# Reordering the start, thinning one bias sum and splitting the last eviction of a tuned Fourier-mixing and expert kernel

## The chip, the cores and the metric

One core of one Trainium2 chip. The metric is device time in microseconds (us), median over executions; a profiled execution gives a trace, whose span is about 1.8 us shorter than the time of the same execution, as it leaves out the launch. All runs told of here were of state fast, or single runs, with a mean granted clock of TensorE of 0.994 or more. Even so, the runs of the kernel before lie in two clusters on every chip used, at 853.0 to 853.9 and 854.5 to 855.9, so a difference of 0.1% needs several runs and an interval.

## The reference, cut to what matters

```python
# x: (8, 3008, 256) float32; out: (24064, 256) float32
X = np.fft.rfft(x, axis=1)                  # along the 3008 positions
Yr = Xr @ w_r - Xi @ w_i + b_r              # 256 x 256, complex
Yi = Xr @ w_i + Xi @ w_r + b_i
Y  = soft_threshold(Yr, 0.01) + 1j * soft_threshold(Yi, 0.01)
x  = np.fft.irfft(Y, n=3008, axis=1).reshape(24064, 256)
h  = x @ w_in                               # 256 x 2048
g  = s * np.maximum(h, 0)**2 + b            # s, b scalars
out = g @ w_out                             # 2048 x 256
```

As b is a scalar, `b @ w_out` is b times the column sums of w_out: one row, added to every row of the result. Those sums are the "bias" of this text.

Names that come up again: x is loaded by batch, so "the third x" is the input of the third batch. F_c and T_c are the tables of the forward and the inverse transform, and the first F matmul (L432, L433 in the changed kernel) is the first that uses F_c and the result of the mixing by W. ring, vd and vs are buffers of later transform stages. `us`, set in this type, is a tile of the kernel and not the microsecond; in the quoted texts, "us" with no figure ahead of it means this tile. A cold array is one for which the trace shows a granted clock of 0.5.

## The kernel before

The transform of 3008 is split into 94 x 32. Batch 0 goes through it by itself, in the head (0 to 52 us). From then on TensorE works through tiles of 512 tokens (first matmul by w_in, Relu on ScalarE, square on VectorE, second matmul by w_out), and the transforms of the next batches are slipped in between as units, at slots of a plan. One slot is one of the 16 slices of the first matmul.

The first stage of batch 0, with W (w_r and w_i) loaded only after the first chunk has been copied:

```python
    def first_batch():
        ut = ypool.tile([P, DC, 96, N2], F16, name="ut", tag="yt")
        keep_awake(36)                           # idle matmuls that warm the array
        for c in range(N2 // XCH):               # 4 chunks of x
            for dc in range(DC):
                ps = two_banks()
                for j in range(XCH):
                    ... matmul(ps[:, j // 4, ...], x16[(0, c)][...], A_t ...)
                for h in range(2):               # two copies out of one two-bank tile
                    evac(ut[:, dc, :, n2 : n2 + 4], ps[:, h, 0:384]...)
            keep_awake(14 if c < 3 else 10)
            if c == 0:
                ... memset(st[0:1, :, 0:D:P], 0.0)   # holds W until VectorE is here
                emit_load_w()
            if c == 1: ... emit_load_forward()       # F_c
            if c == 2: ... emit_load_inverse()       # T_c
            if c == 2: place_w(0)
        place_w(1)
        ...
```

The bias, the second matmul's end and the plan (cuts marked with dots):

```python
    def make_bias():
        ps = other_bank()
        for q in range(MC):                      # 16 matmuls of 256 columns
            nc.tensor.matmul(ps[:, 0:D], ones, w_out_t[:, q, :],
                             start=(q == 0), stop=(q == MC - 1))
        ...
        def mm(sub, mc):                         # a sub-tile is 128 tokens
            h = sub % 2                          # two sub-tiles share a bank
            ...
            if mc == MC - 1 and (h == 1 or sub == nsub - 1):
                ... one VectorE instruction takes both out, then one store each
    ...
    plan.setdefault(15, []).append(make_bias)
    plan.setdefault(17, []).append(lambda: emit_load_x(2))   # third batch
    schedule(22, 44, s23_units(1))                           # second batch
```

The first stage of the second batch (s1_units) writes its result u to DRAM in four stores (ud) and reads it back in another layout in four loads (`us`); this way out and back is called the bounce of u. s23_units(1) starts with matmuls on `us`:

```python
            if j == XCH - 2:
                nc.sync.dma_start(out=ud[:, c * XCH : (c + 1) * XCH, :], in_=u[0:96])
            if i == N2 // 2 - 1:
                for q in range(4):
                    nc.sync.dma_start(out=t, in_=uv[:, 6 * q : 6 * q + 6, :])   # us
```

Of the kernel before, what the change touches and what calls it, by code (L numbers as in the profile page):

```python
# [9 lines left out]
F16 = mybir.dt.float16  # L10
F32 = mybir.dt.float32
# [3 lines left out]
P = 128  # L15
# [81 lines left out]
def kernel(  # L97
# [69 lines left out]
    def two_banks():  # L167
        return hpool.tile([P, 2, 512], F32, name="psh", tag="psh")
# [11 lines left out]
    def emit_load_x(b):  # L180
        xv = x[b].rearrange("(n1 n2) d -> n1 (n2 d)", n2=N2)
        for c in range(N2 // XCH):
            t = xpool.tile([P, XCH * D], F16, name="x16", tag="x16")
            nc.gpsimd.dma_start(  # L184
                out=t[0:N1, :], in_=xv[:, c * XCH * D : (c + 1) * XCH * D]
            )
            x16[(b, c)] = t

    ones = cpool.tile([P, P], F16, name="ones")
# [2 lines left out]
    def keep_awake(n):  # L192

        ps = other_bank()
        for _ in range(n):
            nc.tensor.matmul(ps[:, 0:P], ones, ones, start=True, stop=True)


    A_t = cpool.tile([P, 96], F16, name="A_t")
# [3 lines left out]
    w_st = []  # L203
    for w in (w_r, w_i):
        st = rpool.tile([P, DC, D], F32, name="w_st", tag="rt")
        w_st.append(st)

    def emit_load_w():

        for e in (slice(0, P), slice(P, D)):  # L210
            for w, st in zip((w_r, w_i), w_st):
                nc.sync.dma_start(
                    out=st[:, :, e], in_=w.rearrange("(c p) e -> p c e", p=P)[:, :, e]
                )


    b_g = cpool.tile([P, 2, D], F32, name="b_g")
    nc.vector.memset(b_g, 0.0)
# [52 lines left out]
    nc.vector.memset(T_t, 0.0)  # L271
    F_2 = [uspool.tile([P, H, P], F16, name="F_2", tag="us") for _ in range(2)]
    for f in F_2:
        nc.vector.memset(f, 0.0)

    def make_bounds():
        for t, c in ((low, -LAM), (high, LAM)):
            nc.gpsimd.tensor_scalar(
                out=t, in0=b_st, scalar1=-1.0, scalar2=c, op0=ALU.mult, op1=ALU.add
            )  # L280
# [8 lines left out]
    def blocks(t):  # L289
        return t.rearrange("p q (r a k) -> p q r a k", r=2, a=2)  # L290

    def place_w(ec):
        e = slice(ec * P, ec * P + P)
        for i in range(2):
            nc.scalar.copy(out=W_t[:, :, i, e], in_=w_st[i][:, :, e])

    def place_f(h):
        q = slice(h * H, h * H + H)
# [14 lines left out]
    def place_t(h):  # L313
        q = slice(h * H, h * H + H)
        for i in range(4):
            r = slice(32 * i, 32 * i + 32)
            c = 64 * (i % 2)
            nc.vector.tensor_copy(out=T_t[r, q, c : c + 64], in_=T_c[r, q])

    def make_bias():  # L320
        ps = other_bank()
        for q in range(MC):
            nc.tensor.matmul(
                ps[:, 0:D], ones, w_out_t[:, q, :], start=(q == 0), stop=(q == MC - 1)
            )
        for j in range(2):
            nc.scalar.activation(
                out=bias_bc[:, j], in_=ps[:, 0:D], func=AF.Copy, scale=bb_bc
            )
# [9 lines left out]
    def first_batch():  # L339
        ut = ypool.tile([P, DC, 96, N2], F16, name="ut", tag="yt")  # L340
        last_dve = last_act = None
        keep_awake(36)
        for c in range(N2 // XCH):
            for dc in range(DC):
                ps = two_banks()
                for j in range(XCH):
                    lo = j * D + dc * P
                    last_pe = nc.tensor.matmul(
                        ps[:, j // 4, (j % 4) * 96 : (j % 4) * 96 + 96],
                        x16[(0, c)][0:N1, lo : lo + P], A_t[0:N1, :],  # L350
                        start=True, stop=True,
                    )
                for h in range(2):
                    n2 = c * XCH + 4 * h
                    on_dve, on_act = evac(
                        ut[:, dc, :, n2 : n2 + 4],
                        ps[:, h, 0:384].rearrange("p (n k) -> p k n", k=96), 384,
                    )
                    last_dve = on_dve or last_dve
                    last_act = on_act or last_act  # L360
            with tc.issue_after(last_pe.ins):
                keep_awake(14 if c < 3 else 10)
            if c == 0:
                with tc.issue_after(last_dve.ins):
                    for st in w_st:
                        nc.vector.memset(st[0:1, :, 0:D:P], 0.0)
                emit_load_w()
            if c == 1:
                with tc.issue_after(last_dve.ins):
                    nc.vector.memset(F_c[0:1, 0, 0, 0:1], 0.0)  # L370
                emit_load_forward()
            if c == 2:
                with tc.issue_after(last_dve.ins):
                    nc.vector.memset(T_c[0:1, 0, 0:1], 0.0)
                emit_load_inverse()
            if c == 2:
                with tc.issue_after(last_act.ins):
                    place_w(0)
        with tc.issue_after(last_dve.ins), tc.issue_after(last_act.ins):
            place_w(1)  # L380
            place_f(0)
            place_f_2(0)

# [117 lines left out]
        for i in range(2 * U + 2):  # L501
            if i < 2 * U:
                mix(*steps[i])
            if 0 <= i - 1 < 2 * U:
                fwd_dft(*steps[i - 1])
            if 0 <= i - 2 < 2 * U:
                inv_dft(*steps[i - 2])
            k = i - U - 2
            if 0 <= k < 4:
                turn(0, k)  # L510
            if 0 <= k - 1 < 4:
                last_dft(0, 8 * (k - 1))
            if i >= 2 * U:
                some(3)
            if i == 0:
                with tc.issue_after(g_last[0].ins):
                    place_t(0)
            if i == 1:
                with tc.issue_after(g_last[0].ins):
                    place_f(1)  # L520
            if i == 2:
                with tc.issue_after(g_last[0].ins):
                    place_f_2(1)
            if i == 3:
                with tc.issue_after(g_last[0].ins):
                    place_t(1)
            if i == 9:

                gate = nc.gpsimd.tensor_copy(out=low[0:1, 0, 0:1], in_=vt[0:1, 1, 0, 0:1])
                with tc.issue_after(gate.ins):  # L530
                    make_w_g()
                    make_bounds()
        for k in range(4):
            turn(1, k)
            some(1)
            if k:
                last_dft(1, 8 * (k - 1))
# [269 lines left out]
    def second_mms(ti):  # L807
# [5 lines left out]
        hold = {}  # L813

        def mm(sub, mc):
            h = sub % 2
            if h == 0 and mc == 0:
                hold["ps"] = other_bank().rearrange("p (h e) -> p h e", h=2)
            ps = hold["ps"]
# [4 lines left out]
            )  # L824
            if sub == nsub - 1 and mc % 2 == 1:
                gts.pop((ti, mc // 2))
            if mc == MC - 1 and (h == 1 or sub == nsub - 1):
                k = h + 1
                ost = opool.tile([P, 2, D], F32, name="ost", tag="ost")
                nc.vector.scalar_tensor_tensor(  # L830
                    out=ost[0:size, 0:k], in0=ps[0:size, 0:k], scalar=s_bc[0:size],
                    in1=bias_bc[0:size, 0:k], op0=ALU.mult, op1=ALU.add,
                )
                load["dve"] += 0.12 + 0.27 * k
                for i in range(k):
                    store(tl, sub - k + 1 + i, ost[:, i, :])
# [73 lines left out]
```

## Time and profile before

| | before |
|---|---|
| time, three first runs | 853.37 us median (853.29 to 853.9) |
| span of the profile | 852.0 us |
| TensorE busy | 98% |
| mixing matmuls (L401) run freely from | 16.08 us |
| first unit of the second batch on TensorE | 67.42 us |
| last matmul ends, span ends | 846.76, 852.0 us |

In a profile line, L401 is a line of the kernel, PE is TensorE, PEld its weight loads, DVE VectorE, ACT ScalarE, POOL GpSimd, SPq the queue of DMA issues. "out<-in" are the program's names. A line of the chain reads: start, length, what the end of the program was waiting for at that time. A line of the timeline reads: start, length, engine, instruction, and in brackets the idle time before it and what ended it. The lines of the head, of the first expert tile and of the tail stand in the prediction.

### The profile page before, as it was taken

To read this page: it belongs to the slowest core of one execution; us is meant where nothing else is said; L and a number is where in the kernel's file an instruction comes from. 1 tells how busy PE (TensorE), PEld (TensorE's weight loads), DVE (VectorE), ACT (ScalarE), POOL (GpSimd) and SP (SyncE) were. 2 spreads that over 40 slices of the span, in tenths; PEclk is the share of its full clock that TensorE was granted. 3 is DMA by queue.
4 is the path that set the end of the run, shared out by engine and by line. 5 is a ranking of instruction groups with operands and counts; after the bars stand their busy time and mean duration, and the time that the engine had idled before them with its cause. 6 is when DMAs were issued, how large, how long until landed. Compare 5 with 4: busy or idle time off the path is not lost.

```text
span 852.0 us, 17108 instructions
## 1 busy us (share of the span) xinstructions
PE 836.7 (98%) x6668; PEld 602.7 (71%) x6668; DVE 698.1 (82%) x1027; ACT 643.8 (76%) x860; POOL 32.5 (4%) x54
## 2 busy tenths in 40 slices
PE   8899999999999999999999999999999999999997
PEld 7757777777777766777667776777667777766765
DVE  6888987888878987888878888888977888776674
ACT  5887887787778887787777887787877778666663
POOL 3210000000000000000000000000000000000000
PEclk9999999999999999999999999999999999999999
DMA  7963457424671357424663247613354223411111
GB/s 168 157 155 97 115 138 174 122 77 97 169 195 54 93 151 190 110 78 104 164 159 89 74 106 180 191 39 92 100 155 119 62 78 96 112 32 38 38 44 50
DMA packets 105410, 95.07 MB, mean 112 GB/s; under 512 B 9454, under 2 KB 97778, under 8 KB 103986
## 3 DMA queue, kind: packets, MB, share of 16 engines
q1 hardware_dynamic: 99330, 79.57, 32.3%
q0 software_dynamic: 6000, 14.42, 10.7%
q8 instruction: 52, 0.85, 0.4%
q14 instruction: 28, 0.23, 0.1%
HBM read 52.54 MB, written 46.66 MB: 116 GB/s over the span
## 4 chain that ended last, share of the span: by engine, by line
PE 90%; DVE 4%; ACT 3%; DMA 1%; issue 1%; DVEq 0%; ACTq 0%; POOLq 0%
PE psa L820 37%; PE psh L751 37%; PE psf L617 4%; PE psf L552 3%; PE psf L588 2%; PE psf L603 2%; PE psf L700 2%; PE psf L647 2%; DVE gt L765 1%; ACT rt L758 1%; PE psh L401 1%; DMA w_st<-in_w_r_dram 1%; DMA x<-in_x_dram 1%; ACT yt L160 0%; ACT vs L160 0%
## 5 line engine op out<-in xcount | busy, mean ns | idle before, releaser
L758 ACT ACTIVATE rt<-psh 128x1024 f32<-128x1024 f32 (+2 forms) x384 | 387.1, 1009 | 115.6 <-PE psh L751 114.2
L765 DVE TENSOR_TENSOR gt<-rt 128x1024 f16<-128x1024 f32 (+2 forms) x323 | 386.6, 1200 | 99.4 <-ACT rt L758 98.7
L820 PE MATMUL psa<-w_out_t,gt 128*128 128x256 f16 (+1 forms) x3024 | 453.9, 272 | 0.1
L820 PEld LDWEIGHTS <-gt 128*128 128x128 f16 (+1 forms) x3024 | 301.0, 101 | 186.8 <-issue 1.6
L751 PE MATMUL psh<-yt,w_in 128*128 128x512 f16 (+1 forms) x1344 | 396.9, 378 | 0.0
L751 PEld LDWEIGHTS <-w_in 128*128 128x128 f16 x1536 | 142.8, 98 | 26.6 <-issue 1.7
L830 DVE SCALAR_TENSOR_TENSOR ost<-psa,s_bc,bias_bc 128x512 f32<-128x512 f32 (+1 forms) x96 | 70.9, 738 | 9.6 <-PE psa L820 8.2
L762 ACT ACTIVATE gt<-rt 128x1024 f16<-128x1024 f32 (+2 forms) x61 | 64.1, 1051 | 1.0
L622 DVE TENSOR_TENSOR ring<-psf,s 128x512 f16<-128x512 f32 x84 | 57.5, 685 | 3.5 <-PE psf L617 3.4
L160 ACT CAST v<-psf 128x512 f16<-128x512 f32 x80 | 46.5, 582 | 18.1 <-PE psf L647 18.1
L160 ACT CAST xf<-psf 128x512 f16<-128x512 f32 x82 | 48.0, 585 | 11.1 <-PE psf L588 11.1
L160 ACT CAST u<-psf 96x512 f16<-96x512 f32 x78 | 45.1, 580 | 12.3 <-PE psf L552 12.1
L751 PE MATMUL psh<-tail,w_in 128*128 128x512 f16 (+1 forms) x192 | 52.1, 353 | 0.0
L617 PE MATMUL psf<-W_g,xf 128*128 128x256 f16 x336 | 50.4, 273 | 0.0
L160 ACT CAST yt<-psf 128x480 f16<-128x480 f32 (+2 forms) x76 | 38.5, 518 | 14.4 <-PE psf L700 14.3
L552 PE MATMUL psf<-x,A_t 94*96 94x512 f16 x104 | 39.6, 381 | 1.6 <-ACT yt L160 0.5
L628 DVE TENSOR_TENSOR ring<-ring,high 128x512 f16<-128x512 f16 x84 | 35.5, 423 | 2.2
L629 DVE TENSOR_TENSOR ring<-ring 128x512 f16<-128x512 f16 x84 | 35.5, 422 | 1.9
L627 DVE TENSOR_TENSOR ring<-ring,low 128x512 f16<-128x512 f16 x84 | 35.4, 421 | 1.5
L617 PEld LDWEIGHTS <-xf 128*128 128x128 f16 x336 | 32.9, 98 | 3.7
L184 POOL DMA_DIRECT2D x<-in_x_dram x32 | 16.9, 530 | 461.2 <-PE psf L552 445.1
L700 PE MATMUL psf<-C_t,vs 96*128 96x96 f16 x448 | 32.9, 205 | 0.0
(84 smaller groups left out, 490.7 us busy)
## 6 DMA issues: line engine op xcount, KB each, us to landing
out_dram<-ost SPq DMA_DIRECT2D x152, 128.0 KB
x<-in_x_dram POOLq DMA_DIRECT2D x32, 376.0 KB, 6.0
ud<-u SPq DMA_DIRECT2D x28, 384.0 KB
us<-ud SPq DMA_DIRECT2D x28, 384.0 KB
vd<-v SPq DMA_DIRECT2D x42, 256.0 KB
vs<-vd SPq DMA_DIRECT2D x14, 768.0 KB
ring<-ring SPq DMA_DIRECT2D x280, 32.0 KB
out_dram<-ost SPq DMA_DIRECT2D x16, 120.0 KB
```

Source lines behind the costliest of these rows:

```text
L160: return None, nc.scalar.copy(out=dst, in_=src)
L552: nc.tensor.matmul(ps[0:96, :], A_t[0:N1, :], x16[(b, c)][0:N1, j * D : (j + 2) * D], start=True, stop=True,)
L617: nc.tensor.matmul(ps[:, r, :], xt[:, 2 - r, dc], W_g[:, dc, r], start=(dc == 0), stop=(dc == DC - 1),)
L622: nc.vector.tensor_tensor(out=t, in0=ps, in1=hold[i // 2][:, i % 2].unsqueeze(1).to_broadcast([P, 2, D]), op=ALU.add,)
L628: nc.vector.tensor_tensor(out=m, in0=m, in1=high, op=ALU.min)
L700: nc.tensor.matmul(ps[:, j * 96 : (j + 1) * 96], vs[(b, h)][:, k, ec * P : (ec + 1) * P], C_t, start=True, stop=True,)
L751: nc.tensor.matmul(o, w_in_t[dc][:, mc * P : (mc + 1) * P], r, start=(dc == 0), stop=(dc == DC - 1),)
L758: nc.scalar.activation(out=rt[:, :, 0:w], in_=ps[:, :, 0:w], func=AF.Relu)
L762: nc.scalar.activation(out=gt[:, :, 0:w], in_=rt[:, :, 0:w], func=AF.Square)
L765: nc.vector.tensor_tensor(out=gt[:, :, 0:w], in0=rt[:, :, 0:w], in1=rt[:, :, 0:w], op=ALU.mult)
L820: nc.tensor.matmul(ps[0:size, h, :], gts[(ti, mc // 2)][:, mc % 2, sub * size : (sub + 1) * size], w_out_t[:, mc, :], start=(mc == 0), sto ...
L830: nc.vector.scalar_tensor_tensor(out=ost[0:size, 0:k], in0=ps[0:size, 0:k], scalar=s_bc[0:size], in1=bias_bc[0:size, 0:k], op0=ALU.mult, o ...
```

## The change

Three intents. The head is to lose the wait for W (W goes first, x comes in halves, each group of matmuls has a bank of its own so that ScalarE and VectorE copy side by side). The sixteen bias matmuls are to become one, with the column sums begun on GpSimd. At the end, the last two sub-tiles are to leave PSUM one by one, so that the last eviction and store are half as large.

```diff
@@ emit_load_x
-            nc.gpsimd.dma_start(out=t[0:N1, :], in_=xv[:, c * XCH * D : (c + 1) * XCH * D])
+            parts = 2 if b == 0 else 1
+            w = XCH * D // parts
+            for i in range(parts):
+                nc.gpsimd.dma_start(out=t[0:N1, i * w : (i + 1) * w], in_=...)
@@ W: loaded at once
+        nc.sync.dma_start(out=st, in_=w.rearrange("(c p) e -> p c e", p=P))
-    def emit_load_w(): ...
@@ F_2
-        nc.vector.memset(f, 0.0)
+        nc.gpsimd.memset(f, 0.0)
@@ column sums
+    def sum_w_out():
+        acc = opool.tile([P, 2, D], F32, name="acc", tag="ost")
+        nc.gpsimd.tensor_tensor(out=acc, in0=w_out_t[:, 0:2], in1=w_out_t[:, 2:4], op=ALU.add)
+        for q in range(4, MC, 2):
+            nc.gpsimd.tensor_tensor(out=acc, in0=acc, in1=w_out_t[:, q : q + 2], op=ALU.add)
+        nc.gpsimd.tensor_tensor(out=w_sum, in0=acc[:, 0], in1=acc[:, 1], op=ALU.add)
     def make_bias():
-        for q in range(MC):
-            nc.tensor.matmul(ps[:, 0:D], ones, w_out_t[:, q, :], ...)
+        nc.tensor.matmul(ps[:, 0:D], ones, w_sum, start=True, stop=True)
@@ first_batch
-        keep_awake(36)
+        last_pe = keep_awake(40)
-        for c in range(N2 // XCH):
+        for g in range(N2 // 4):
+            c, h = divmod(g, 2)
             for dc in range(DC):
-                ps = two_banks()
+                ps = one_bank() if dc else two_banks()[:, 0]
                 ... 4 matmuls in place of 8, one copy in place of two
-                keep_awake(14 if c < 3 else 10)
+                last_pe = keep_awake(5)
+            if h == 0:
+                continue
             if c == 0:
-                ... emit_load_w()
-            if c == 1:
                 ... emit_load_forward()          # F_c, now after the first chunk
-            if c == 2:  place_w(0)
+            if c == 1:  place_w()
@@ make_bounds()
+                    sum_w_out()
@@ second_mms
+            alone = ti == len(tiles) - 1 and sub >= 2
-            h = sub % 2
+            h = 0 if alone else sub % 2
-            if mc == MC - 1 and (h == 1 or sub == nsub - 1):
+            if mc == MC - 1 and (alone or h == 1 or sub == nsub - 1):
```

More of the change, by code (lines that the diff above doesn't have):

```diff
@@ L183, in emit_load_x @@
             t = xpool.tile([P, XCH * D], F16, name="x16", tag="x16")
-            nc.gpsimd.dma_start(
-                out=t[0:N1, :], in_=xv[:, c * XCH * D : (c + 1) * XCH * D]
-            )
+            parts = 2 if b == 0 else 1
+            w = XCH * D // parts
+            for i in range(parts):
+                nc.gpsimd.dma_start(
+                    out=t[0:N1, i * w : (i + 1) * w],
+                    in_=xv[:, c * XCH * D + i * w : c * XCH * D + (i + 1) * w],
+                )
             x16[(b, c)] = t
@@ L195, in keep_awake @@
         for _ in range(n):
-            nc.tensor.matmul(ps[:, 0:P], ones, ones, start=True, stop=True)
+            mm = nc.tensor.matmul(ps[:, 0:P], ones, ones, start=True, stop=True)
+        return mm
     A_t = cpool.tile([P, 96], F16, name="A_t")
@@ L205 @@
         st = rpool.tile([P, DC, D], F32, name="w_st", tag="rt")
+        nc.sync.dma_start(out=st, in_=w.rearrange("(c p) e -> p c e", p=P))
         w_st.append(st)
-    def emit_load_w():
-        for e in (slice(0, P), slice(P, D)):
-            for w, st in zip((w_r, w_i), w_st):
-                nc.sync.dma_start(
-                    out=st[:, :, e], in_=w.rearrange("(c p) e -> p c e", p=P)[:, :, e]
-                )
     b_g = cpool.tile([P, 2, D], F32, name="b_g")
@@ L290, in blocks, with place_w @@
         return t.rearrange("p q (r a k) -> p q r a k", r=2, a=2)
-    def place_w(ec):
-        e = slice(ec * P, ec * P + P)
+    def place_w():
         for i in range(2):
-            nc.scalar.copy(out=W_t[:, :, i, e], in_=w_st[i][:, :, e])
+            nc.scalar.copy(out=W_t[:, :, i], in_=w_st[i])
     def place_f(h):
@@ L318, in place_t @@
             nc.vector.tensor_copy(out=T_t[r, q, c : c + 64], in_=T_c[r, q])
+    w_sum = cpool.tile([P, D], F16, name="w_sum")
+    def sum_w_out():
+        acc = opool.tile([P, 2, D], F32, name="acc", tag="ost")
+        nc.gpsimd.tensor_tensor(
+            out=acc, in0=w_out_t[:, 0:2], in1=w_out_t[:, 2:4], op=ALU.add
+        )
+        for q in range(4, MC, 2):
+            nc.gpsimd.tensor_tensor(out=acc, in0=acc, in1=w_out_t[:, q : q + 2], op=ALU.add)
+        nc.gpsimd.tensor_tensor(out=w_sum, in0=acc[:, 0], in1=acc[:, 1], op=ALU.add)
     def make_bias():
         ps = other_bank()
-        for q in range(MC):
-            nc.tensor.matmul(
-                ps[:, 0:D], ones, w_out_t[:, q, :], start=(q == 0), stop=(q == MC - 1)
-            )
+        nc.tensor.matmul(ps[:, 0:D], ones, w_sum, start=True, stop=True)
         for j in range(2):
@@ L341, in first_batch @@
         last_dve = last_act = None
-        keep_awake(36)
-        for c in range(N2 // XCH):
+        last_pe = keep_awake(40)
+        for g in range(N2 // 4):
+            c, h = divmod(g, 2)
             for dc in range(DC):
-                ps = two_banks()
-                for j in range(XCH):
-                    lo = j * D + dc * P
-                    last_pe = nc.tensor.matmul(
-                        ps[:, j // 4, (j % 4) * 96 : (j % 4) * 96 + 96],
-                        x16[(0, c)][0:N1, lo : lo + P], A_t[0:N1, :],
-                        start=True, stop=True,
-                    )
-                for h in range(2):
-                    n2 = c * XCH + 4 * h
-                    on_dve, on_act = evac(
-                        ut[:, dc, :, n2 : n2 + 4],
-                        ps[:, h, 0:384].rearrange("p (n k) -> p k n", k=96), 384,
-                    )
-                    last_dve = on_dve or last_dve
-                    last_act = on_act or last_act
+                ps = one_bank() if dc else two_banks()[:, 0]
+                with tc.issue_after(last_pe.ins):
+                    for j in range(4):
+                        lo = (4 * h + j) * D + dc * P
+                        mm = nc.tensor.matmul(
+                            ps[:, j * 96 : j * 96 + 96],
+                            x16[(0, c)][0:N1, lo : lo + P], A_t[0:N1, :],
+                            start=True, stop=True,
+                        )
+                last_pe = mm
+                on_dve, on_act = evac(
+                    ut[:, dc, :, 4 * g : 4 * g + 4],
+                    ps[:, 0:384].rearrange("p (n k) -> p k n", k=96), 384,
+                )
+                last_dve = on_dve or last_dve
+                last_act = on_act or last_act
             with tc.issue_after(last_pe.ins):
-                keep_awake(14 if c < 3 else 10)
+                last_pe = keep_awake(5)
+            if h == 0:
+                continue
             if c == 0:
-                with tc.issue_after(last_dve.ins):
-                    for st in w_st:
-                        nc.vector.memset(st[0:1, :, 0:D:P], 0.0)
-                emit_load_w()
-            if c == 1:
                 with tc.issue_after(last_dve.ins):
@@ L375, in first_batch @@
                 emit_load_inverse()
-            if c == 2:
+            if c == 1:
                 with tc.issue_after(last_act.ins):
-                    place_w(0)
+                    place_w()
         with tc.issue_after(last_dve.ins), tc.issue_after(last_act.ins):
-            place_w(1)
             place_f(0)
```

## The prediction

> **What bounds the kernel now.** I read the page's busy table first, then the chain that ended last, then, because the change touches only the head (0 to 18 us), the first expert tile (52 to 64 us) and the tail (843 to 852 us), the ordered chain and the timeline of those three stretches.
>
> ```profile
> PE 836.7 (98%) x6668; PEld 602.7 (71%) x6668; DVE 698.1 (82%) x1027; ACT 643.8 (76%) x860; POOL 32.5 (4%) x54
> ...
> PE 90%; DVE 4%; ACT 3%; DMA 1%; issue 1%; DVEq 0%; ACTq 0%; POOLq 0%
> ```
>
> TensorE is 98% busy and 90% of the chain, so the body (64 to 838 us) is bound by matmuls. I compared the order of instructions of the two kernels engine by engine: away from the three places nothing is added or moved. So the body should take what it takes, and the gain is that of head, first tile and tail, at most some 2% of the time together.
>
> The head, from the chain in order of time:
>
> ```profile
> 1.21 4.85 DMA x<-in_x_dram
> 6.11 1.48 PE psh L348 x16
> 7.61 0.49 ACT ut L160
> 8.12 0.56 DVE ut L164
> 8.73 4.99 DMA w_st<-in_w_r_dram
> 15.00 1.03 DVE ut L164 x2
> 16.08 1.82 PE psh L401 x15
> ```
>
> The mixing matmuls (L401) run freely from 16.08. What they wait for is the last two copies of ut on VectorE (15.00 to 16.03). Those wait for ScalarE, which stood before W, in order, until W landed at 13.72. W was issued only at 8.73, behind the first chunk's copies.
>
> ```profile
> 10.25 1.14 DVE L164 CAST ut<-psh 128x384 f16<-128x384 f32 x2 [1.56 <-ACT ut L160]
> 11.96 1.09 DVE L164 CAST ut<-psh 128x384 f16<-128x384 f32 x2 [0.57 <-ACT ut L160]
> ```
>
> VectorE waits here for ScalarE's copy, not for TensorE, although they copy different banks: the two halves of one tile are taken in turn.
>
> How busy the DMA engines are with x, in the DMA view of 6.0 to 8.5 us, and with W in that of 10.5 to 11.5 us:
>
> ```profile
> q0 software_dynamic: 150, 0.53, 105.5%
> ```
>
> ```profile
> q1 hardware_dynamic: 445, 0.22, 72.8%
> q0 software_dynamic: 80, 0.03, 19.9%
> ```
>
> x alone fills all 16 engines from 3.5 to about 10.5 us. So once W no longer holds, x itself is the next limit.
>
> The tail:
>
> ```profile
> 841.56 5.21 PE psa L820 x46
> 846.79 0.75 DVE ost L830
> ```
>
> The last matmul ends at 846.76, one 512-column eviction takes 0.75, and the span ends at 852.0. The stores take 0.60 us each to issue (row of ost on the SP queue, 603/616/1292 ns), the last from 848.2.
>
> **What the Trainium skill says.** "TensorE: Matmul & The Clock Gate", section "The HAM clock gate", gives a gap of 107 ns for 128-column matmuls on a cold array and 56 ns on a warm one. The trace agrees: of the 36 warm-up matmuls the first starts at 1.04 and the last at 4.75, 106 ns apart, and after 10 us fourteen take 0.8 us. "PSUM — Partial Sum Buffer", section "Specifications (TRN2)", says that ScalarE and VectorE can read PSUM in parallel so long as they are not in one bank; the head doesn't do so today, as the waits above show. "DMA: Bandwidth & Descriptors", section "Queues, rings and completion order", says that each engine goes round robin between queues by packet. The trace is compatible (both queues move data at 10.5 to 11.5) but doesn't prove the order. "GPSIMD Engine Reference", section "Elementwise — side-by-side cycle accounting", has a two-input add of 2048 columns at 4497 ns, 2.2 ns a column; here the W_g add of 128x512 took 1.263 us, 2.5 ns a column, and I use that.
>
> **The change part by part.**
>
> 1. *Head.* Removed: the hold on W. W (0.52 MB) is now issued at about 1.1 us, before x has packets on the engines (about 2.5 us). Eight issues of half chunks take 8 x 0.53 = 4.3 us of GpSimd instead of 2.2, still ahead of the data. Warm-up matmuls: 36 + 52 = 88 become 40 + 40 = 80; the first 40 at 106 ns end at 5.3 us. Clearing F_2 (1.5 us) goes from VectorE to GpSimd.
> What replaces the wait is the stream of x. Estimate: x filled the engines from 2.5 to about 10.6, 8.1 us. At 11.5 to 12.5 us W's queue alone moved 0.25 MB in a microsecond at 90%, with 512 B packets; with 1 KB packets I take 1.3 to 1.8 us of engine time for W. Some 0.5 us of that fits before x starts. So x ends 0.8 to 1.3 us later, at 11.4 to 11.9. F_c is now released earlier: after the second chunk's VectorE copies, about 10 us, against 11.44. Its 0.39 MB (about 1.4 us of engine time) shares the engines with the last half chunk and puts off x by another 0.4 to 0.9. So x's last byte is at about 12.5, and its semaphore at about 13.6, as the first chunk showed some 1.1 us between its bytes having moved (about 4.9, summing the GB/s row) and TensorE's start at 6.1. Then 8 matmuls of 59 ns = 0.5, and one VectorE copy of 0.53 with 0.1 of handing over: mixing from about 14.75 in place of 16.08. Gain 1.3, likely 0.6 to 2.6. The rest of the head (18 to 52 us) is a dependent chain through all three engines and moves along with its start; T_c (issued 13.10, landed by 17.24, used at 18.20) has 1 us to spare and is issued about a microsecond earlier as well.
>
> 2. *Column sums.* Sixteen matmuls of 0.109 us (L323 in the chain: 0.44 + 0.44 + 0.87 = 1.75 us) become one: 1.64 us less TensorE work. GpSimd gains 7 x 1.26 + 0.65 = 9.5 us, from when w_out has landed (issue 21.09 plus 18.2 = 39.3, less the shift) to about 48, well before the bias matmul at some 56; x of the third batch, next in its queue, is late by 2 us with tens to spare. But TensorE isn't the only full engine there:
>
> ```profile
> 56.87 1.08 ACT L758 ACTIVATE rt<-psh 128x1024 f32<-128x1024 f32 x1
> 57.79 0.64 ACT L160 CAST u<-psa 96x512 f16<-96x512 f32 x1
> 58.25 2.01 ACT L758 ACTIVATE rt<-psh 128x1024 f32<-128x1024 f32 x2
> 60.46 1.02 ACT L758 ACTIVATE rt<-psh 128x1024 f32<-128x1024 f32 x1 [0.20 <-PE psh L751]
> 61.82 0.84 ACT L327 ACTIVATE bias_bc<-psa,bb_bc 128x256 f32<-128x256 f32 x2 [0.33 <-PE psa L323]
> ```
>
> ScalarE runs without a gap from 53.2 to 60.3. psh has two buffers, so the matmuls for the sixth activation need the fourth done at 57.9, and they ran at 58.0: the first 0.44 of bias work was hidden, and the second nearly so. Only the last 0.87 stood in the way. In the new order ScalarE's two bias copies (0.84 us) come between activations 6, 7 and 8, where ScalarE is the limit. Following both engines by hand, activation 7 ends at about 61.6 (after 60.2 for the sixth and 0.42 for a bias copy), and the ninth's matmuls start there in place of 62.05. Gain 0.45 to 0.95; I take 0.6 of the 1.64.
>
> 3. *Tail.* Sub-tiles 2 and 3 leave separately. The last eviction has 256 columns, 0.476 us (shortest of that row) for 0.75: 0.27. One store is left to issue after it, not two: 0.60. The last 128 KB no longer queue behind another 128 KB, 0.7 us at the 188 GB/s seen there: up to 0.4 more. The bank that sub-tile 3 needs is free at 844.5, before its first matmul (846.76 - 16 x 0.109 = 845.0), so no new wait. Gain 0.9 to 1.4; I take 1.2.
>
> Sum: 1.3 + 0.6 + 1.2 = 3.1 us of 853.37, 0.4%: 850.2.
>
> **The rivals.**
>
> *W's transfer only pushes x back by what it saves.* For it: the engines are full with x, and W and F_c now come before x's last bytes. Then the head gains 0 to 0.5, and the kernel takes about 851.3. Against it: 0.5 us or more of W goes before x, and the double serialisation on ScalarE is gone in any case.
>
> *The head is freed altogether.* If W's packets slip into x's gaps at no cost, x lands at about 11.8, mixing starts at 13 and the head gains 3; with 1.6 from the bias and 1.2 from the tail the time is 847.6. Against it: x took more than 100% of the engines.
>
> *GpSimd becomes the bound or slows VectorE.* Its sum holds the SBUF path from 38 to 47 us. Against it: VectorE's additions of g at 34 to 39, beside GpSimd's W_g, took the same 1.2 us as elsewhere. Should it hold, I would expect 1 us back at most.
>
> *The body pays for it.* A shift against the DMA stores could change waits like the vd one at 110 us (2.29 us). The whole plan moves together, so I allow 0.4 us either way.
>
> **Range and chances.** The three parts range over 0.6 to 2.6, 0.4 to 1.6 and 0.9 to 1.4; with the body's 0.4 the sum is 1.6 to 4.8 us for eight in ten: 848.6 to 851.8. A gain of 2% would be 17 us, more than the head could ever give up to mixing, and no part could cost 17 us. Faster 0.004, same 0.992, slower 0.004.
>
> **What would show it.** Right: the first long run of L401 starts at 14 to 15.3, with W's copies on ScalarE in the middle of ut's and no wait for W, and TensorE waits for DMA x several times; ut copies of ScalarE and VectorE overlap; one L329 matmul, and ScalarE without a gap until the first tile's last activation; the last eviction about 0.48 and one store behind it, the span ending some 4.1 us after the last matmul (5.2 now). Wrong: mixing at 13 (x not held back) or after 15.6 (held back in full), VectorE's durations up while GpSimd adds, or a new wait of TensorE on w_sum.

## The result

| | runs | median (range) | ratio to before, 95% interval |
|---|---|---|---|
| before | 6 | 854.37 us (853.29 to 855.13) | |
| changed | 6 | 855.19 us (854.58 to 856.53) | 1.0013 [1.0000, 1.0026] |

A ratio here and below is the mean time of one kernel's fast runs over the mean of the other's from the same rounds, so not quite the ratio of the medians. The change gains nothing: it costs about 1 us where 3.1 were forecast as a gain.

The profile of the changed kernel, busy times and shares of the chain (first lines of the page):

```profile
PE 836.0 (98%) x6645; PEld 600.3 (70%) x6645; DVE 697.2 (82%) x1024; ACT 643.5 (75%) x858; POOL 46.0 (5%) x68
...
PE 89%; DVE 4%; ACT 3%; DMA 3%; issue 1%; POOL 0%; DVEq 0%; ACTq 0%; SPq 0%; POOLq 0%
```

TensorE is busy 0.7 us less and the span is 1.1 us longer. The chain's share of DMA has gone from 1% to 3%: some transfer is waited for now that was hidden. The head of the changed kernel, from its timeline:

```profile
13.60 0.34 PE L354 MATMUL psh<-A_t,x 94*128 94x96 f16 x4 [0.84 <-DMA x<-in_x_dram]
...
14.52 1.95 PE L402 MATMUL psh<-W_t,ut 128*128 128x256 f16 x16
```

The last half chunk of x is waited for until 13.60 and mixing starts at 14.52, 1.56 us before the 16.08 of the kernel before. Not all of that lasts. The first copy of the mixing result on ScalarE, before and changed:

```profile
17.93 1.01 ACT L408 CAST g<-psh 128x1024 f16<-128x1024 f32 x1 [0.35 <-PE psh L401]
```

```profile
15.15 1.67 ACT L297 COPY F_t<-F_c 64x768 f16<-64x768 f16 x2 [0.69 <-DMA F_c<-dft_fwd]
16.85 1.01 ACT L409 CAST g<-psh 128x1024 f16<-128x1024 f32 x1
```

Before, this copy waits for the matmuls. In the changed kernel it waits behind two copies of F_c, which landed only at 15.07; it starts 1.08 us earlier. The place where the time goes is the start of the second batch. The chain of the kernel before there:

```profile
66.98 0.44 PE psa L820 x4
67.42 0.22 PE psf L588 x4
67.64 0.43 PE psh L751 x2
68.08 0.44 PE psa L820 x4
...
69.60 0.57 PE psf L603 x4
```

And of the changed kernel (L590 is L588 of before, L605 is L603, L753 is L751, L824 is L820):

```profile
57.37 5.60 DMA ud<-u
...
63.13 4.37 DMA us<-ud
67.49 0.05 issue
67.54 0.40 PE psf L590 x4
67.94 0.54 PE psh L753 x2
68.47 0.85 PE psa L824 x4
69.33 0.43 PE psf L590 x4
69.75 0.85 PE psh L753 x2
70.61 0.85 PE psa L824 x4
71.46 0.54 PE psf L605 x4
72.00 0.43 PE psh L753 x2
```

In the kernel before TensorE simply goes on. In the changed kernel the chain leaves TensorE: it runs over the last store of u, the first load of `us` and only then back to the first unit. The timeline puts the wait at 2.37 us. Most matmuls after it take twice as long as the same ones in the fence above, up to 71.5: 0.85 against 0.43 and 0.44. Taking each excess (0.18 + 0.11 + 0.41 + 0.21 + 0.42 + 0.41) gives 1.74 us more. (L605 shows no excess: its 0.54 compares with 0.57 in the kernel before. The expectation of e3 below still has 1.84 and 4.2, with 0.10 for it.) The trace's own record of the clock agrees. In this line, from the view by windows for 68.13 to 71.54, the third number from the end is the granted clock:

```profile
68.13:71.54 3.41, 3.41 (x18) 2.17 (x16) 0.63 (x3) 1.91 (x3) 0.00 (x0) 0.50 0.53 141
```

Half of 3.41 us is 1.7. Wait and cold array together cost 4.1 us.

With these the first pair of traces adds up. The unit could have started at 65.16 (64.56 + 0.60, the end of the matmuls before it) for 67.42 before, a lead of 2.3 us; it loses 2.4 and 1.7; from the third of these groups (71.04 and 72.87) to the last matmul the two kernels take 775.7 and 776.0, 0.2 more; the tail gains 1.0. That makes +1.0, and the spans differ by 1.1. So the time isn't lost elsewhere in the body.

What the transfers compete with is the load of the third x. From 57.5 to 60 us, while the last store of u is under way, the queue of x takes 77.9% of the 16 DMA engines' time in the changed kernel and that of the stores 20.1%. The issues on GpSimd, before:

```profile
46.51 0.64 POOL L184 DMA_DIRECT2D x<-in_x_dram  x1 [7.13 <-PE psa L552]
48.31 0.52 POOL L184 DMA_DIRECT2D x<-in_x_dram  x1 [1.16 <-PE psa L552]
```

and changed:

```profile
39.69 7.32 POOL L324 TENSOR_TENSOR acc<-acc,w_out_t 128x512 f32<-128x512 f32 x6
46.95 0.64 POOL L187 DMA_DIRECT2D x<-in_x_dram  x1
```

Before, GpSimd sat idle and issued the load as soon as TensorE had freed the buffer. In the changed kernel everything is 1.1 us earlier, but the sums hold the queue until 46.95, so this load is 0.4 us later in time and 1.5 us later against the rest. The issues of the stores of u and the loads of `us` (SP queue), before and changed:

```profile
46.85 11.90 SPq L559 DMA_DIRECT2D ud<-u  x4
62.01 3.20 SPq L566 DMA_DIRECT2D us<-ud  x4
```

```profile
45.78 11.90 SPq L561 DMA_DIRECT2D ud<-u  x4
63.13 3.21 SPq L568 DMA_DIRECT2D us<-ud  x4
```

The stores are issued 1.1 us earlier; the first load of `us`, which needs the last store landed, 1.1 us later. As the last store's issue begins about 0.3 us before the end of its row, it took 3.6 us before and 5.8 us changed. The tail, from the chain of the changed kernel:

```profile
843.62 5.21 PE psa L824 x46
...
848.85 0.48 DVE ost L834
```

From the end of the last matmul (848.82) to the end of the span (853.1) it is 4.3 us, in place of 5.2.

### The profile page after: what moved, and what is told of

Its sections match the earlier page's. It is cut to its first block, busy times and chain, and to the rows that moved or that the text cites. A ratio compares the mean times of both kernels' runs of the same rounds, so it can differ in the third digit from the quotient of the medians.

```text
span 853.1 us, 17069 instructions
## 1 busy us (share of the span) xinstructions
PE 836.0 (98%) x6645; PEld 600.3 (70%) x6645; DVE 697.2 (82%) x1024; ACT 643.5 (75%) x858; POOL 46.0 (5%) x68
## 4 chain that ended last, share of the span: by engine, by line
PE 89%; DVE 4%; ACT 3%; DMA 3%; issue 1%; POOL 0%; DVEq 0%; ACTq 0%; SPq 0%; POOLq 0%
PE psa L824 37%; PE psh L753 36%; PE psf L619 4%; PE psf L554 3%; PE psf L590 2%; PE psf L605 2%; PE psf L649 2%; PE psf L702 2%; DVE gt L767 1%; ACT rt L760 1%; DMA F_c<-dft_fwd 1%; DMA ud<-u 1%; DMA x<-in_x_dram 1%; DMA us<-ud 1%; ACT yt L160 1%
## 5 line engine op out<-in xcount | busy, mean ns | idle before, releaser
L824 PE MATMUL psa<-w_out_t,gt 128*128 128x256 f16 (+1 forms) x3024 | 455.1, 273 | 0.1
L824 PEld LDWEIGHTS <-gt 128*128 128x128 f16 (+1 forms) x3024 | 301.3, 101 | 187.8 <-issue 2.4
L753 PE MATMUL psh<-yt,w_in 128*128 128x512 f16 (+1 forms) x1344 | 397.3, 378 | 0.3 <-ACT rt L760 0.3
L753 PEld LDWEIGHTS <-w_in 128*128 128x128 f16 x1536 | 142.9, 98 | 27.4 <-issue 2.1
L834 DVE SCALAR_TENSOR_TENSOR ost<-psa,s_bc,bias_bc 128x512 f32<-128x512 f32 (+2 forms) x97 | 71.0, 732 | 9.9 <-PE psa L824 8.5
L624 DVE TENSOR_TENSOR ring<-psf,s 128x512 f16<-128x512 f32 x84 | 57.5, 684 | 3.7 <-PE psf L619 3.2
L753 PE MATMUL psh<-tail,w_in 128*128 128x512 f16 (+1 forms) x192 | 52.1, 353 | 0.0
L187 POOL DMA_DIRECT2D x<-in_x_dram x36 | 19.0, 531 | 455.0 <-PE psf L554 448.3
L590 PE MATMUL psf<-F_t,us 128*128 128x128 f16 x336 | 32.7, 220 | 2.4 <-DMA us<-ud 2.4
```

The costliest lines, as they stand in the source:

```text
L590: nc.tensor.matmul(ps[:, :, dc, j, :], t[:, q, dc * P : (dc + 1) * P], F_t[:, 2 * i + j, :], start=True, stop=True,)
L624: nc.vector.tensor_tensor(out=t, in0=ps, in1=hold[i // 2][:, i % 2].unsqueeze(1).to_broadcast([P, 2, D]), op=ALU.add,)
L753: nc.tensor.matmul(o, w_in_t[dc][:, mc * P : (mc + 1) * P], r, start=(dc == 0), stop=(dc == DC - 1),)
L824: nc.tensor.matmul(ps[0:size, h, :], gts[(ti, mc // 2)][:, mc % 2, sub * size : (sub + 1) * size], w_out_t[:, mc, :], start=(mc == 0), sto ...
L834: nc.vector.scalar_tensor_tensor(out=ost[0:size, 0:k], in0=ps[0:size, 0:k], scalar=s_bc[0:size], in1=bias_bc[0:size, 0:k], op0=ALU.mult, o ...
```

## The experiments

Theory S: head, sums and tail each gain what they should, but TensorE then reaches the second batch before `us` has landed, and the sums make `us` land later. The rivals were that the head gains nothing that lasts, that the landing of `us` is fixed by bandwidth alone, and that the time is lost elsewhere in the body.

### e1 and e2: the head alone, head and tail

e1 is the changed kernel without its column sums and without its tail; e2 has head and tail. Edit against the changed kernel:

```diff
-        nc.tensor.matmul(ps[:, 0:D], ones, w_sum, start=True, stop=True)
+        for q in range(MC):
+            nc.tensor.matmul(ps[:, 0:D], ones, w_out_t[:, q, :], ...)
-                    sum_w_out()
-            alone = ...                         # e1 only
```

> Only the head of the change on the kernel before (x in half chunks, W first, F_2 cleared on GpSimd); column sums and tail as before. Theory S (the gains are real, but TensorE then reaches the first unit that reads us before us has landed; GpSimd's sums make it worse by starting the load of the third x 1.5 us late): without the sums the third x starts with the head, the bounce of u through DRAM too, us lands some 1 us earlier than before's 66.4, TensorE needs it at 66.2, no wait over 0.5 us: 1.1 us faster than before, ratio 0.9987. Rival D (the landing of us is set by DMA bandwidth and does not follow the head): TensorE waits 0.5 to 1.5 us at that unit, ratio 0.9995 to 1.0005. Rival H (the head itself gains nothing that lasts): ratio 1.000 without any wait for us.

> The change without the column sums: head and tail. Theory S: the gains of head and tail add up, 1.1 + 0.9 = 2.0 us, ratio 0.9977, no wait for us over 0.5 us, and last matmul to end of span 4.3 us in place of 5.2. Rival D: the wait for us is there with 0.5 to 1.5 us, ratio 0.9985 to 0.9995.

e1: 853.91 us against 854.55, ratio 0.9996 [0.9984, 1.0009]. e2: 852.79, ratio 0.9983 [0.9970, 0.9995]. Neither profile has a wait for `us`; the last store of u took 3.6 to 3.8 us. So without the sums the wait is absent in these two traces, and the tail is worth the difference, 0.0013 or 1.1 us. The head is worth only about 0.3 us, and that isn't clear of noise: e1 missed its forecast of 0.9987, and fits rival H (nothing that lasts) as well as a small gain. The start of mixing shows why: in e1 it was 15.74, in e2 15.06. Over the eight traces with this head (the changed kernel twice, e1 to e4, e6 and e7) it lies between 14.52 and 16.15, mean 15.3. Over the six with the head of before (twice itself, e5, e11, e13, e14) it lies between 15.38 and 16.08, mean 15.7. The first profile of before was at the late end, the first of the changed kernel at the early end. At the first F matmul even this is gone: it comes at 17.93 in the mean of the six and at 17.97 in the mean of the eight. One reason is in the traces: in e1 the array is cold while it mixes (granted clock 0.50 from 14.5 to 17.5; the 16 matmuls take 2.89 us for 1.95), and in e6 before it (0.50 from 8.5 to 15.0).

### e3: the second batch four slots later

```diff
-    schedule(22, 44, s23_units(1))
+    schedule(26, 40, s23_units(1))
```

> The changed kernel with the units of the second batch starting four slots later (26 over 40 in place of 22 over 44), so that TensorE needs us 3.5 to 4 us later. Theory S: the wait for us (2.37 us) and the cold matmuls after it (1.84 us) go: 853.1 - 4.2 = 848.9 for the span, ratio to before 0.9964. Rival P (the time is lost elsewhere in the body, or the later units crowd what follows): the wait goes but the ratio stays at 0.999 to 1.001.

853.36 us, ratio 0.9992 [0.9978, 1.0006]; the forecast of 0.9964 was missed. The wait for `us` is gone, though the last store was as slow (5.8 us). But some 2 us are lost again later: the chain now passes through copies of ring (3.20 us) at 90 us and a store of vd (2.45 us) at 109, of which the kernel before has the second too (2.29 us at 110), and the order of many instructions has changed. Moving the user isn't free; the transfer has to be moved.

### e4: the third x held until us has landed

```diff
-    plan.setdefault(17, []).append(lambda: emit_load_x(2))
+    gate_t = cpool.tile([P, 1], F16, name="gate_t")
+    def gated_load_x2():
+        gate = nc.gpsimd.tensor_copy(out=gate_t[0:1], in_=us[(1, 3)][0:1, 0, 0:1])
+        with tc.issue_after(gate.ins):
+            emit_load_x(2)
+    plan.setdefault(17, []).append(gated_load_x2)
```

Every other engine keeps the order of the changed kernel.

> The changed kernel with the load of the third x held on GpSimd until us has landed, so that nothing competes with the bounce of u through DRAM. Theory S in its form that the third x is what slows the bounce: the last store of u takes 3 us or less in place of 5.6, us lands before 65, no wait, ratio to before 0.9964. Rival R (the bounce is slow by its own bytes and receipts): us lands after 66.5 still, TensorE waits over 1 us, ratio 0.999 to 1.0013.

851.73 us, ratio 0.9970 [0.9958, 0.9983], against 1.0013 for the changed kernel. From its SP queue:

```profile
47.06 11.89 SPq L561 DMA_DIRECT2D ud<-u  x4
61.77 2.15 SPq L568 DMA_DIRECT2D us<-ud  x4
```

The last store takes 3.1 us with nothing of x beside it, and there is no wait. What the parts gain now reaches the end, and the third x, 23 us later, is early enough still. In this trace the head was the slowest of all (mixing at 16.15), so its span of 850.6 is no good case.

### e5: the column sums alone

The kernel before with sum_w_out and the one-matmul bias, nothing else.

> The column sums on GpSimd alone, on the kernel before (head and tail as before). Theory S (the sums hold GpSimd until about 48, so the load of the third x starts 1.5 us late, falls on the last store of u, and us lands after TensorE wants it): TensorE reaches the first unit about 66.2 and waits 2 to 2.5 us for us, then runs cold for some 1.8 us; against a gain of 1.05 us from the matmuls the kernel is 2.5 to 3.5 us slower, ratio 1.003 to 1.004. Rival G (the sums only take work from TensorE): ratio 0.9988, no wait. Rival M (it is the three parts together that make TensorE early): wait under 0.5 us, ratio 0.999.

856.34 us, ratio 1.0018 [0.9999, 1.0037], less than forecast in the mean because the runs split: two at 853.0 and 853.2, no slower than the fastest of before (853.2), and four at 856.3 to 858.6. The profiled one, of the four, waited 2.3 us for `us` and then ran slow to 72.3. So the sums, which only take work from the busiest engine, make the kernel slower in four of six runs.

### e6: the sums cut in two

After five of the eight additions the first load of the third x is issued, then the rest follows. Only the order on GpSimd changes.

```diff
-        for q in range(4, MC, 2):
+        for q in range(4, 12, 2):
             nc.gpsimd.tensor_tensor(out=acc, in0=acc, in1=w_out_t[:, q : q + 2], op=ALU.add)
+    def end_sum_w_out():
+        load = emit_load_x(2, range(1))
+        with tc.issue_after(load.ins):
+            ... the additions of 12 and 14, then w_sum
```

> The changed kernel with the sums on GpSimd cut in two, so that the first load of the third x is issued 2 to 2.5 us earlier (after five of the eight additions) and the rest of the sums follows it; every other engine has the same order. Theory S: the last store of u takes 4 us or less in place of 5.6, TensorE waits under 1 us for us and does not go cold, ratio to before 0.997 to 0.998 (0.3 to 0.4% better than the changed kernel). Rival D (the landing of us depends on the number of bytes in flight, not on when the first load starts): wait 2 us or more, ratio 1.000 to 1.002.

851.79 us, ratio 0.9985 [0.9965, 1.0004], for a forecast of 0.997 to 0.998. Four runs at 850.9 to 851.8, two at 854.1 and 856.2. In the profile the last store took 3.9 us and nothing waited. The load was no longer held by the sums: it came at 46.38, when TensorE freed the buffer. So with an earlier start of this one load the wait is gone in the trace. In the other runs it can only be guessed from the times: that at 856.2 has a mean clock of 0.994, that at 854.1 one of 1.000, so what the latter lost isn't a cold array. The interval overlaps that of the changed kernel, so the gain over it isn't clear of noise.

### e7: a warm array through the wait

```diff
+    def stay_warm(n):
+        ps = one_bank()
+        for _ in range(n):
+            nc.tensor.matmul(ps[:, 0:P], ones, ones, start=True, stop=True)
+    plan.setdefault(22, []).append(lambda: stay_warm(40))
```

> The changed kernel with 40 idle matmuls of 128 columns before the first unit of the second batch (34 of them, some 1.9 us, right where TensorE waits for us). If the 1.84 us after the wait are the cost of a cold array: the matmuls after the wait take 0.22 us a pair of 512 columns less, the wait itself becomes under 0.7 us and the ratio to before falls from 1.0013 to about 0.9993. If the slow matmuls after the wait have another cause (operands, contention): ratio 1.001 to 1.0015.

853.70 us, ratio 0.9995 [0.9984, 1.0007], 0.18% or 1.5 us better than the changed kernel (the intervals overlap a little), all five runs within 0.25 us. From its chain:

```profile
63.70 4.04 DMA us<-ud
67.74 0.05 issue
67.79 0.40 PE psf L590 x4
68.19 0.43 PE psh L753 x2
68.62 0.43 PE psa L824 x4
```

`us` lands as late as in the changed kernel, but the matmuls after it take 0.43, and the mean clock of this trace is 1.000. So the slow matmuls of the changed kernel were a cold array, and about 1.5 of its 4.1 us can be had back with idle work that computes nothing.

### e8: F_c released later, besides e4

```diff
-            if c == 0:
+            if c == 2:
                 with tc.issue_after(last_dve.ins):
                     nc.vector.memset(F_c[0:1, 0, 0, 0:1], 0.0)
                 emit_load_forward()
```

> As e4_x2_after_us, and F_c released only after the third chunk (with T_c), so that it no longer shares the DMA engines with most of x. If F_c is what holds the last half chunk of x: that lands about 1 us earlier (mixing at 13.3 to 14.0 in place of 14.5 to 16.2), ratio 0.9960 to 0.9967 against 0.997 of e4. If F_c then becomes the wait (ScalarE and VectorE wait for it over 1 us and the first F matmul is no earlier than 17.3): ratio 0.997 to 0.998.

851.18 us, ratio 0.9964 [0.9952, 0.9976]. Mixing starts at 14.43. The first F matmul comes at 17.73, within what the other new heads have (17.34 to 19.18), as F_c now lands later: ScalarE waited 1.63 us for it. That is the wait of the second forecast with the ratio of the first. The step from e4 is inside the noise. In its chain a copy of ring beside the third x takes 7.47 us and TensorE waits about 0.3 us for it: e4's hold moves some of the contention.

### e9 and e10: before and changed once more

> The kernel before once more, for a second trace, as its runs fall into two clusters (853.0 to 853.5 and 854.6 to 855.4). If the clusters come from the head (landing of the last x and W, or a cold array): mixing starts at 16.1 or some 1.3 us later, and the body after 67 us is the same to 0.2 us. If they come from the bounce of u: the first unit waits 1 us or more for us in the slow one.

> The changed kernel once more, for a second trace. Theory S: the wait of TensorE for us (2.4 us in the first trace) and cold matmuls after it are there again, 1.5 to 3.5 us and 1.5 to 2 us. Rival: the first trace caught a rare event, and here there is no wait.

e9: 853.27 us, span 851.5, mixing from 15.40, a single run of the fast cluster. So it could not tell what the slow one is, and that stays open. It showed something else: its last store of u took 5.4 us, and `us` still landed in time (first load issued at 63.14, used at 66.58). Had that load taken the 4.37 us of the changed kernel, TensorE would have waited some 0.9 us, so the slow store alone doesn't make the wait. e10: 855.20 us; TensorE waited 2.9 us for `us` and ran slow until 71.4. The first trace was no accident.

### e11: the hold of e4 on the kernel before

> Control: the kernel before with nothing but the load of the third x held until us has landed. If the hold only removes the wait that the change made: ratio 0.9995 to 1.0005. If the hold is a gain of its own (the kernel before waits for us too in some runs): ratio 0.998 to 0.999, and its runs lie closer together.

854.70 us, ratio 1.0010 [0.9997, 1.0024]. The hold is no gain of its own. What it brings on the changed kernel is the removal of the wait that the change had made.

### e12: the third x held for the first quarter of us only

e8 with `us[(1, 0)]` in place of `us[(1, 3)]` in the gate.

> As e8, but the third x is held only until the first quarter of us has landed, so that it is through before the copies of ring start. In e8 the first ring copies took 7.5 us beside it and TensorE waited 0.4 us for them. If that costs: ring copies under 4 us, ratio 0.9955 to 0.9962. If it is of no account: 0.9964 as in e8. If x slows the other quarters of us: TensorE waits for us again, ratio over 0.997.

850.63 us (850.05 to 851.16), ratio 0.9961 [0.9949, 0.9974]: better than both kernels by more than 3 us, correct, and with no wait for `us` and none for the copies of ring near 76 us; mixing started at 13.77. The step from e8 (0.9964) is inside the noise. This is the version to keep.

### e13 and e14: a late load without an early TensorE, and the reverse

e13 is the kernel before with the sums made and not used. e14 has one bias matmul on a slice of w_out and no sums (a wrong result, relative error 0.60).

```diff
# e13: the sixteen bias matmuls stay
+                    sum_w_out()
# e14: no sum_w_out
-        for q in range(MC): ...
+        nc.tensor.matmul(ps[:, 0:D], ones, w_out_t[:, 0, :], start=True, stop=True)
```

> The kernel before with the sums made on GpSimd but not used (the sixteen bias matmuls stay): a late load of the third x without an earlier TensorE. If the late load is what slows the bounce: the last store of u takes 5 to 6 us (3.6 in the first trace of before), us lands about 68 and TensorE, there at 66.7 to 67.4, waits 0.5 to 1.5 us in many runs; ratio 1.0005 to 1.002. If it is of no account: store about 3.6 us, ratio 0.9995 to 1.0003.

> The kernel before with one bias matmul on the first slice of w_out in place of sixteen and no sums on GpSimd (wrong result on purpose): an earlier TensorE without a late load. If the late load is needed for the wait: the store takes about 3.6 us in most runs, no wait or under 0.5 us, 1.3 us gained, ratio 0.9983 to 0.9988. If an early TensorE is enough: wait over 1 us and cold matmuls, ratio 1.001 to 1.003 as in e5.

e13: 854.65 us, ratio 1.0000 [0.9986, 1.0014]: the slow store of its first forecast, with the ratio of its second. e14: 853.73 us, ratio 0.9995 [0.9981, 1.0008], short of its forecast of 0.9983 to 0.9988. The SP queue of e13, then of e14:

```profile
46.55 11.90 SPq L571 DMA_DIRECT2D ud<-u  x4
63.36 2.50 SPq L578 DMA_DIRECT2D us<-ud  x4
```

```profile
46.45 11.90 SPq L556 DMA_DIRECT2D ud<-u  x4
61.94 2.17 SPq L563 DMA_DIRECT2D us<-ud  x4
```

With the same start of the stores, the first load of `us` comes 1.3 us later in e13, with the idle sums, than in e14 (5.2 us for the last store against 3.9). One pair of traces can't show that the sums did it, as e9 had 5.4 without any. Over all twelve traces in which x is loaded beside the store it is plainer: the six with the sums ahead of the load have 5.2 to 6.0 us, five of the six others 3.6 to 3.9, and the sixth is e9. TensorE, which comes at 67.11 in e13, doesn't notice. In e14 it comes at 65.83, and `us` is there. Neither half by itself makes the wait in its profile; e5 has both, and waits 2.3 us. e14 gained only about 0.4 us in the mean where its trace shows 1.2, and its runs spread over 2.5 us; that some of them waited for `us` is likely, but no trace of such a run exists.

## Why the prediction was wrong

| part | forecast | measured | from |
|---|---|---|---|
| head | -1.3 | 0 to -0.4 | e1 -0.3, not clear of noise; mean start of mixing 15.7 to 15.3, of the first F matmul 17.9 to 18.0 |
| sums, on TensorE | -0.6 | -1.2 | first F matmul to first unit: 67.42 - 18.34 = 49.08 before, 48.98 with the new head alone (e1, e2), 66.10 - 18.32 = 47.78 in e6 |
| tail | -1.2 | -1.0 | 5.2 to 4.3 us after the last matmul; e2 against e1 1.1 |
| new wait for `us` | 0.4 either way | +2.4 and +1.7 cold | first trace; 2.9 of wait in e10, 2.3 in e5 |
| sum | -3.1 | +1.5 to +1.9, ratio says +1.1 | means and first trace mixed; the first pair alone adds up to +1.0 |

1. **The body.** The step that failed is "away from the three places nothing is added or moved. So the body should take what it takes", and with it the sentence that the third x "is late by 2 us with tens to spare". Both look at instructions. The order of instructions indeed did not change, and the third x indeed wasn't needed for a long time. But its transfer shares the DMA engines with the bounce of u, and the change spends the time by which that bounce comes ahead of TensorE. The rival "the body pays for it" was named and given 0.4 us; it was 4.1. I had not compared how long before its use `us` lands in the kernel before. That is the number that would have warned: its first load is issued at 62.01, and one takes 4.4 us in the changed kernel, so it lands near 66.4 by that estimate, for a use at 67.3. (It may land earlier: that of e9 took at most 3.4 us.) Two of the gains, head and sums, were to bring this use forward by 1.9 us by my own figures. None of the signs that the prediction listed looked there: mixing at 14.52, one L329 matmul and a last eviction of 0.48 all came as it said, and it was wrong.

2. **The cold array.** Nothing in the prediction has it, though it quotes the two speeds. A wait of 2.4 us cost 1.7 us more afterwards; the granted clock of 0.50 and e7 show that it was the clock.

3. **The head.** Up to mixing the mechanism held: x itself was the limit, with several waits for DMA x, and mixing in the first trace began at 14.52 for a forecast of 14.75. That the rest "moves along with its start" did not hold: F_c took 0.5 us of it away in that trace, and a cold array more in e1, which the working with 59 ns a matmul leaves out. The rival that gave the head 0 to 0.5 was nearer. The size was off also because both ends were taken as fixed. The start of mixing in the kernel before was read from one trace, at the late end of its range, and the landing of the last x varies by over 1 us between runs. One detail was misread: F_c is released after the first chunk's copies (8.11), not after the second's at about 10. It landed at 15.07, and e12 mixes earliest of all with F_c behind the third chunk.

4. **The sums' gain** was mis-sized the other way. By hand I let TensorE stand while ScalarE was the limit; the compiled order had moved twelve matmuls by w_out of the first tile into those gaps (five at 57.78, three at 60.10 and at 61.36, one at 62.20 in the changed kernel, where before the first came at 62.48). The order of instructions had shown them and I didn't count them. The true gain is 1.2 of the 1.64 us.

5. **The tail** held, term by term: eviction 0.48 for 0.75, one store of 0.6 us fewer to wait for.

6. **GpSimd against VectorE.** The rival of a shared path did not show: an addition of g on VectorE beside the sums (from 39.33) took 1.21 us, as did the same one before (from 40.40).

What stays open: the two clusters of the kernel before (a hint: of 38 of its runs with a clock, 17 of the 19 below 854.2 us have 0.999, and 17 of the 19 above have 0.994 to 0.997, so the slow ones had more of the cold array; where, no trace shows), the 2 us that e3 loses later, and why the last store of u takes 5.4 us in one of the two traces of before without any sums. That the third x is what slows the store is shown by e4, e8, e11 and e12, in all of which it takes 3.1 us; why it suffers more in one run than in another isn't.

## What to carry to other kernels

Before taking work off the busiest engine, list the transfers whose results it uses next and how long before their use they land: a gain larger than that slack turns into a wait, and here the wait brought a cold array as well. An engine that only issues loads isn't free: work put on it can delay the next load (here by 1.5 us), and that load can fall on a transfer that does matter. List signs of being wrong for the parts that the change does not touch, too. When the parts of a change add up to a gain that the whole doesn't show, run the parts crossed, as e13 and e14 do: each half can be harmless alone.

## What the Trainium skill lacked or had wrong

- "TensorE: Matmul & The Clock Gate", "The HAM clock gate": it has the array cold again after an idle window of about 3.4 us, and its section "Why this matters for your kernels" advises no gaps of more than some 3 us. Here gaps of 2.37 us (changed kernel) and 2.3 us (e5) were enough for 3.4 us at a granted clock of 0.50; filled with idle matmuls down to 0.3 us (e7), no slow matmul followed.
- "GPSIMD Engine Reference", "Elementwise — side-by-side cycle accounting": the rate is near, 1.22 us for an addition of 512 columns (7.32 for six, 2.4 ns a column; the page's figure gives 2.2).
- None of the pages read has what one store costs beside another load: the same 384 KB store of u to DRAM took 3.1 us by itself (four traces), and between 3.6 and 6.0 us beside the load of x (twelve traces).
